# Forming the down weights' combinations early and spooling them, instead of forming them when the MLP starts

## The chip, the cores and the metric

The kernel runs on one core of one Trainium2 chip. The metric is device time in microseconds (us) of one execution. Three runs of the kernel before took 1996.1, 1996.38 and 1999.25 us, so the median is 1996.38 us. The profile that is quoted below is one execution of its own, whose span is 1997.3 us.

Five engines work side by side: TensorE (PE, matrix products), VectorE (DVE), ScalarE (ACT), GpSimd (POOL) and SyncE (SP). In this kernel SP issues every transfer.

## What is computed

The reference is one transformer block with conditioned layer norms, on x of 8192 positions by D = 448 channels:

```
m  = silu(c) @ w_mod                       # six rows: sa, ca, ga, sb, cb, gb
h  = layernorm(x) * (1 + ca) + sa
f  = rfft(h, over the 8192 positions)
f  = soft_shrink(W2 * relu(W1 * f + b1) + b2, 0.01)   # complex, four blocks of 112 channels
x  = x + ga * irfft(f)
h  = layernorm(x) * (1 + cb) + sb
y  = (gelu(h @ w_gate) * (h @ w_up)) @ w_down          # F = 1792 hidden channels
out = x + gb * y
```

The change concerns `w_down`, a matrix of 1792 by 448.

## The kernel before, in words

**Three stages.** Stage A loads x, takes the layer norm statistics and does the first part of the transform. Stage B is a software pipeline of 32 spectral units, `step(0)` to `step(31)`, followed by `drain()`. A unit of about 8.5 us does, for different units at once: `fetch_t` (two transfers `tr<-td` for the unit two steps ahead), `stage_s2` and `stage_m1` (the first complex product), `stage_m2` and `split_y` (the second product; `t` and `y` on DVE, L429 and L437, then `yh` on ACT, L101, and `yl` on POOL, L103), and `stage_i1` (the inverse transform, stored by `vd<-us`). Each exact product uses a high and a low half of its operand, so every operand is split by a cast (high, `zh`, `hh`, `yh`, `th`) and by a subtraction (low, `zl`, `hl`, `yl`, `tl`). The call `at(unit, hook, function)` places other work into a unit. The hook "load" comes right after the unit's fetch and "act" before its `stage_m2`. The hook "dve" comes after its last `split_y` and ahead of `stage_m1`. In this way the units also load and scale `w_gate` and `w_up` (L629, L734, and L743 on DVE in every second unit).

**The seam.** After `drain()` comes a stretch that prepares the first chunk of the MLP: the row ga and the row gb (L609), the last inverse transform (L917 to L919), the residual (L928, L929), statistics, the second norm (`norm2`, L968, L969), the packing into halves (`pack_hi` L974 on ACT, `pack_lo` L981 to L983) and transposes on TensorE (`ptr`, L1001) with their copies (`nt`).

**The MLP.** It runs over 32 chunks of 256 positions. In each chunk `gate_up(i, k)` for k = 0 to 13 does the products with `w_gate` and `w_up` (`pgu`, L1019), then the gelu on ACT (L1055), the product `x` on DVE (L1060), the combinations of `x` on POOL (L1066 to L1069) and the two halves `ac` (L1077 on ACT, L1078 on DVE). A group of output banks in PSUM is reused four values of k later, so TensorE waits for `x` when DVE is late by more than that. At k = 2 of the next chunk `down(i)` multiplies by `w_down` in the Strassen manner: a block of 2 by 2 parts is done with seven products instead of eight. For this each of the seven pairs t of 128-row blocks of `w_down` needs seven matrices of 128 by 224: the four parts, of which three are used as they are, and four combinations of them. Each is needed as a high and a low half in fp16. The fp16 tile `wds[t]` holds them.

**Preparing the next chunk.** While a chunk's `gate_up` runs, the next chunk's inverse, residual, norm, packing and transposes are placed behind certain values of k by a table: `first` for the first chunk, `second` for the second, `hooks` for all the others. The small steps of a reciprocal square root (L112 to L121) are fed one by one between other DVE work.

**The down weights before.** Units 2, 4, ... 14 load `w_down` once (L749) only to take each row's largest absolute value (L753). Units 18 and 19 turn these into one scale per row (`dsc`). The weights are loaded a second time for the preparation proper (L793). For pair t, `parts_hi` (ACT, three instructions, L829 to L831) scales the raw weights and casts the parts. `parts_lo` (six instructions, L835 to L841) subtracts and forms the four combinations. `sums_hi` (ACT, L844) and `sums_lo` (L848) split those. Pairs 0 and 1 are prepared after `drain()` and in the seam, mostly on POOL, and pairs 2 to 6 in the table `first`, on ACT, DVE and POOL, during the first chunk and into the second. The space of the tiles `dr` of L793 comes free only when the seam's last `sums_lo` (DVE, L848) is done.

All transfers stand in one order on SP. They rotate over eight completion semaphores, so a transfer is not issued before the one eight places ahead of it has landed.

Of the kernel before, what the change touches and what calls it, by code (L numbers as in the profile page):

```python
# [43 lines left out]
def spectral_geglu(ctx, tc, x, w1, b1, w2, b2, wg, wu, wd, cvec, wmod, cf1, cs2, cmi, cgm, out):  # L44
# [252 lines left out]
    with ExitStack() as bctx:  # L297
# [493 lines left out]
        def load_d(raw, t):
            raw = raw[:, : 2 * D].rearrange("p (q c) -> p q c", q=2)
            dma(raw, wd.rearrange("(q t p) c -> t p q c", q=2, p=128)[t])  # L793
            return raw

        def load_d4(pool, t):
            draws[t] = load_d(raw_tile(pool).rearrange("p q c -> p (q c)"), t)
# [25 lines left out]
        def quarters(t):  # L823
            r = draws[t]
            return [r[:, q, h * HC : (h + 1) * HC] for q in range(2) for h in range(2)]

        def parts_hi(t):
            r, w = draws[t], wds[t]
            S.activation(r, r, AF.Copy, scale=dsc[:, t : t + 1])  # L829
            S.copy(w[:, 0, 0:2], r[:, :, 0:HC])  # L830
            S.copy(w[:, 0, 2], quarters(t)[3])  # L831

        def parts_lo(t, el=V, add=None):
            w, (b11, b12, b21, b22) = wds[t], quarters(t)
            el.tensor_tensor(w[:, 1, 0:2], draws[t][:, :, 0:HC], w[:, 0, 0:2], ALU.subtract)  # L835
            el.tensor_tensor(w[:, 1, 2], b22, w[:, 0, 2], ALU.subtract)
            add = add or el
            add.tensor_tensor(b11, b12, b11, ALU.subtract)
            add.tensor_tensor(b12, b22, b12, ALU.subtract)
            add.tensor_tensor(b22, b22, b11, ALU.subtract)  # L840
            add.tensor_tensor(b21, b21, b22, ALU.subtract)  # L841

        def sums_hi(t):
            S.copy(wds[t][:, 0, 3:7], draws[t].rearrange("p q (h c) -> p (q h) c", h=2))  # L844

        def sums_lo(t, el=V):
            w, r = wds[t], draws.pop(t).rearrange("p q (h c) -> p (q h) c", h=2)
            el.tensor_tensor(w[:, 1, 3:7], r, w[:, 0, 3:7], ALU.subtract)  # L848

        def down_weights(t, el=V, add=None):  # L850
            parts_hi(t)
            parts_lo(t, el, add)

        def down_weights2(t, el=V):
            sums_hi(t)
            sums_lo(t, el)
# [26 lines left out]
    with ExitStack() as cctx:  # L883
# [265 lines left out]

        first = {  # L1150
            0: [(split_g, 1), (split_v, 1), (parts_hi, 2)],
            2: [(inverse, 1), (parts_hi, 3), (residual, 1), (parts_lo, 2, V, V)],
            3: [(sums_hi, 2), (stats2, 1)],
            4: [(rsqrt_part, 1, 5), (parts_hi, 4), (sums_lo, 2, G), (load_d8, 5), (rsqrt_part, 1, 4)],
            5: [(parts_lo, 3, V, G), (rsqrt_part, 1, 5)],
            7: [(sums_hi, 3), (sums_lo, 3, V), (load_d8, 6)],
            8: [(norm2, 1, 0), (norm2, 1, 1), (parts_lo, 4, G, G), (parts_hi, 5)],
            10: [(pack_hi, 1), (parts_lo, 5, V, V), (pack_lo, 1), (sums_hi, 4)],
            11: [(sums_lo, 4, G), (transposes, 1, 0), (transposes, 1, 2), (sums_hi, 5)],
            12: [(transposes, 1, 4), (sums_lo, 5, G), (parts_hi, 6), (transposes, 1, 6)],  # L1160
            14: [(parts_lo, 6, V, V), (sums_hi, 6)],
            15: [(sums_lo, 6, G)],
        }
# [123 lines left out]
```

## Time and profile before

| what | value |
|---|---|
| runs | 1996.1, 1996.38, 1999.25 us (median 1996.38) |
| profiled execution, span | 1997.3 us |
| TensorE busy | 1930.8 us, 97% of the span |
| DVE, ACT, POOL busy | 1154.4, 772.0, 1190.8 us |
| spectral units | to about 384 us, then the last ones drain |
| seam | about 403 to 424 us |
| chunk 0 of the MLP | about 424 to 474 us |
| steady MLP | from about 510 us |

The busy share of TensorE is close to all of the span, but its ends are modelled. What a stretch really did is better seen from the number of matmuls in it and from the granted clock beside them. A view by windows gives, for each stretch, the busy time of each engine with the number of its instructions in brackets, then the granted TensorE clock (1.00 is full speed), the share of the time in which the transfer engines were busy, and GB/s. A view of waits gives, for each engine and line, the idle time that ended when another engine's instruction ended: the sum, how often, and the longest.

### The profile page before, as it was taken

How to read it: one execution, taken by the hardware profiler on the slowest of the kernel's cores; microseconds unless marked ns; L12 is line 12 of the kernel's file. 1: busy time of each engine (PE TensorE's matmuls, PEld its weight loads, DVE VectorE, ACT ScalarE, POOL GpSimd, SP SyncE). 2: the span in 40 equal slices, each digit the busy share in tenths (PEclk: the TensorE clock that was granted, in tenths of full speed). 3: DMA queues.
4: the chain of work that ended last, by engine and by line, in shares of the span. 5: the costliest groups of instructions: out<-in, count | busy, mean ns of one | idle time of the engine just before them, and what ended most of it. 6: DMA issues, size and time to landing. Idle time of an engine off the chain costs nothing.

```text
span 1997.3 us, 43616 instructions
## 1 busy us (share of the span) xinstructions
PE 1930.8 (97%) x17678; PEld 1712.6 (86%) x17678; DVE 1154.4 (58%) x2419; ACT 772.0 (39%) x1307; POOL 1190.8 (60%) x1478
## 2 busy tenths in 40 slices
PE   7889989987999999999999999999999999999999
PEld 3588989966898888888888888888888888889898
DVE  8468888867555555555554555555555555555533
ACT  5555667653333333333333333333333333333322
POOL 3234446557666666666666666666666666666644
PEclk9889999988999999999999999999999999999999
DMA  9996657721111111111111111111111111111000
GB/s 351 325 227 173 170 147 198 192 89 46 47 44 43 43 43 43 44 49 42 42 49 47 42 42 42 42 51 42 42 42 42 42 43 43 43 43 43 22 17 19
DMA packets 165697, 157.72 MB, mean 79 GB/s; under 512 B 86516, under 2 KB 146552, under 8 KB 165496
## 3 DMA queue, kind: packets, MB, share of 16 engines
q1 hardware_dynamic: 165496, 154.95, 27.4%
q8 instruction: 138, 2.26, 0.5%
q14 instruction: 63, 0.52, 0.1%
HBM read 95.09 MB, written 44.04 MB: 70 GB/s over the span
## 4 chain that ended last, share of the span: by engine, by line
PE 83%; DVE 8%; DMA 4%; ACT 2%; SPq 1%; POOL 1%; issue 1%; DVEq 0%; ACTq 0%; POOLq 0%
PE pgu L1019 51%; PE pdn L1087 7%; PE pdn L1085 7%; PE pdn L1086 7%; DVE y L437 2%; PE ps L194 1%; DMA xt<-in_A_x 1%; DMA raw<-in_B_w_up 1%; DVE zl L352 1%; DMA td<-xt 1%; PE pi L919 1%; DVE hl L407 1%; DVE t L429 1%; PE pi L917 1%; PE pi L918 1%
## 5 line engine op out<-in xcount | busy, mean ns | idle before, releaser
L1019 PE MATMUL pgu<-nt,wh 128*128 128x256 f16 x6272 | 835.2, 273 | 1.2 <-DVE x L1060 1.2
L1019 PEld LDWEIGHTS <-wh 128*128 128x128 f16 x6272 | 603.2, 98 | 99.4 <-issue 31.3
L1055 ACT ACTIVATE gel<-pgu,dg 128x256 f32<-128x256 f32 x448 | 199.8, 471 | 789.8 <-PE pgu L1019 750.0
L1019 PE MATMUL pgu<-nt,wl 128*128 128x256 f16 (+1 forms) x3584 | 502.6, 273 | 0.5 <-DVE x L1060 0.4
L1085 PE MATMUL pdn<-wd,ac 128*128 128x224 f16 x1568 | 407.8, 260 | 4.3 <-DVE x L928 2.3
L1087 PE MATMUL pdn<-wd,ac 128*128 128x224 f16 x1568 | 407.8, 260 | 0.2 <-DVE ac L1078 0.2
L1086 PE MATMUL pdn<-wd,ac 128*128 128x224 f16 x1568 | 407.7, 260 | 0.0
L1066 POOL TENSOR_TENSOR x<-x 128x128 f32<-128x128 f32 x223 | 240.2, 1077 | 234.6 <-DVE x L1060 234.6
L1078 DVE SCALAR_TENSOR_TENSOR ac<-x,sa_act,ac 128x896 f16<-128x896 f32 (+1 forms) x225 | 311.6, 1385 | 81.8 <-ACT ac L1077 81.8
L1019 PEld LDWEIGHTS <-wl 128*128 128x128 f16 (+1 forms) x3584 | 298.2, 97 | 58.3 <-issue 24.8
L1060 DVE TENSOR_TENSOR x<-pgu,gel 128x256 f32<-128x256 f32 x448 | 179.4, 418 | 282.9 <-ACT gel L1055 282.2
L1077 ACT ACTIVATE ac<-x,sa_act 128x896 f16<-128x896 f32 (+1 forms) x225 | 233.0, 1035 | 53.1 <-POOL x L1069 51.2
L1120 POOL TENSOR_TENSOR o<-u,p 128x224 f32<-128x224 f32 x32 | 21.0, 656 | 292.8 <-DVE u L1119 292.8
L1067 POOL TENSOR_TENSOR x<-x 128x128 f32<-128x128 f32 x223 | 158.4, 710 | 17.5
L1086 PEld LDWEIGHTS <-ac 128*128 128x128 f16 x1568 | 154.1, 98 | 5.5 <-issue 4.7
L1085 PEld LDWEIGHTS <-ac 128*128 128x128 f16 x1568 | 154.0, 98 | 1.0 <-issue 0.2
L1087 PEld LDWEIGHTS <-ac 128*128 128x128 f16 x1568 | 154.0, 98 | 0.9 <-DVE ac L1078 0.5
L103 POOL TENSOR_TENSOR yl<-y,yh 128x448 fp32r<-128x448 f32 x63 | 75.3, 1196 | 89.1 <-ACT yh L101 86.8
L1068 POOL TENSOR_TENSOR x<-x 128x128 f32<-128x128 f32 x223 | 112.2, 503 | 0.0
L103 POOL TENSOR_TENSOR tl<-tr,th 128x896 f16<-128x896 f32 x30 | 57.3, 1909 | 87.5 <-ACT th L101 74.4
L1069 POOL TENSOR_TENSOR x<-x 128x128 f32<-128x128 f32 x223 | 108.0, 484 | 0.0
L437 DVE TENSOR_TENSOR y<-pm,t 64x224 f32<-64x224 f32 x256 | 99.5, 389 | 8.1
(305 smaller groups left out, 2835.7 us busy)
## 6 DMA issues: line engine op xcount, KB each, us to landing
tr<-td SPq DMA_DIRECT2D x64, 224.0 KB, 4.8
vd<-us SPq DMA_DIRECT2D x64, 224.0 KB, 3.0
xx<-in_A_x SPq DMA_DIRECT2D x32, 448.0 KB, 3.4
v<-vd SPq DMA_DIRECT2D x64, 224.0 KB, 2.9
out<-x SPq DMA_DIRECT2D x31, 448.0 KB, 2.6
xt<-in_A_x SPq DMA_DIRECT2D x15, 896.0 KB, 17.5
nt<-pk SPq DMA_TRANSPOSE x480, 2.3
td<-xt SPq DMA_DIRECT2D x8, 896.0 KB, 15.7
```

Of the source, the lines that this page charges most:

```text
L103: (el or V).tensor_tensor(lo, src, h, ALU.subtract)
L437: V.tensor_tensor(y[ri * 64 : ri * 64 + 64, gi], pv[si, ri], tv[si, ri], ALU.subtract)
L1019: T.matmul(pgu[i, t, q][:, pr * H : (pr + 1) * H], w[rows, tw, f0 : f0 + 128], nts[i][rows, tn, :], start=start, stop=stop, skip_group_che ...
L1055: S.activation(gl, ps[:, :H], AF.Gelu_apprx_tanh, scale=dg)
L1060: V.tensor_tensor(dst, ps[:, H : 2 * H].rearrange("p (b c) -> p b c", b=2), gl.rearrange("p (b c) -> p b c", b=2), ALU.mult)
L1066: e.tensor_tensor(s1, a21, a22, ALU.add)
L1067: e.tensor_tensor(s2, s1, a11, ALU.subtract)
L1077: S.activation(ac[:, 0, k], x[:, k], AF.Copy, scale=sc)
L1078: V.scalar_tensor_tensor(ac[:, 1, k], x[:, k], sc, ac[:, 0, k], op0=ALU.mult, op1=ALU.subtract)
L1085: T.matmul(ps, ac[:, 0, ka], wds[t][:, 0, kb], start=t == 0, stop=False)
L1086: T.matmul(ps, ac[:, 0, ka], wds[t][:, 1, kb], start=False, stop=False)
L1087: T.matmul(ps, ac[:, 1, ka], wds[t][:, 0, kb], start=False, stop=t == NP - 1)
```

## The change

The combinations are now formed in fp32 from the raw weights during units 4 to 16, before any scale is known, and stored.

- A new DRAM buffer `wdd` holds for each of the seven pairs a block of 128 by 7 by 224 in fp32 (784 KB). `load_m` loads the four parts of a pair by three transfers into a tile `m`, in units 4, 6, 7, 9, 11, 12 and 14. One unit later `down_sums` takes the row maximum on DVE (over 896 values to one column, where two columns were made before) and forms the four combinations on POOL. One more unit later `store_m` stores all seven matrices to `wdd`.
- The preparation of a pair is then a load of its block (`load_d`), one ACT instruction `down_hi` (scale and cast of 128 by 1568) and one DVE instruction `down_lo` (scale and subtract of 128 by 1568).
- For pairs 0 to 2 (`ND = 3`) these are placed in units 22 and 23, 25 and 26, 28 and 29. For pairs 3 to 6 they are placed in the table `first`, by k. Nothing of the down weights is left between `drain()` and the first chunk except two loads.
- The table `first` is rearranged: the next chunk's norm comes at k = 5 and 6 (before at 8), the packing at 6 and 8 (before at 10), the transposes at 10, 11 and 12 (before at 11 and 12).
- Two of the four combinations change places in the block, so two products in `down` swap their index. The number of matmuls stays.
- The scratch space that the program sets aside for software-generated transfers is made smaller. All of the kernel's transfers are of the hardware kind.

```diff
+ND = 3
+    wdd = dram.tile([NP, 128, 7, HC], F32, name="wdd")
...
-            raw = raw_tile(pool).rearrange("p q c -> p (q c)")[:, : 2 * D].rearrange("p (q c) -> p q c", q=2)
-            dma(raw, wd[j * 256 : (j + 1) * 256, :].rearrange("(q p) c -> p q c", p=128))
+            m = pool.tile([128, 7, HC], F32, tag="m", name="m", bufs=4)
+            r = wd.rearrange("(q t p) c -> t p q c", q=2, p=128)[t]
+            dma(m[:, 0:2], r[:, :, :HC])
+            dma(m[:, 3], r[:, 0, HC:])
+            dma(m[:, 2], r[:, 1, HC:])
...
+        def down_sums(t):
+            m = raws[("m", t)]
             V.tensor_reduce(
-                dn[:, 2 * j : 2 * j + 2], raws.pop(("m", j)), mybir.AxisListType.X, ALU.max, apply_absolute_value=True
+                dn[:, t : t + 1], m[:, 0:4].rearrange("p q c -> p (q c)"), mybir.AxisListType.X, ALU.max, apply_absolute_value=True
             )
+            b11, b21, b22, b12, c1, c4, c3 = (m[:, j] for j in range(7))
+            G.tensor_tensor(c1, b12, b11, ALU.subtract)
+            G.tensor_tensor(c3, b22, c1, ALU.subtract)
+            G.tensor_tensor(c4, b21, c3, ALU.subtract)
+            G.tensor_tensor(b12, b22, b12, ALU.subtract)
+        def store_m(t):
+            dma(wdd[t], raws.pop(("m", t)))
...
-        for j in range(7):
-            at(2 + 2 * j, "load", pre, npool, ("m", j), load_m, j)
-            at(3 + 2 * j, "dve", down_max, j)
+        for t, n in enumerate((4, 6, 7, 9, 11, 12, 14)):
+            at(n, "load", pre, npool, ("m", t), load_m, t)
+            at(n + 1, "dve", down_sums, t)
+            at(n + 2, "load", store_m, t)
...
+        def load_d(pool, t, bufs):
+            draws[t] = pool.tile([128, 7, HC], F32, tag="dr", name="dr", bufs=bufs)
+            dma(draws[t], wdd[t])
...
+        def down_hi(t):
+            assert not tiny
+            S.activation(wds[t][:, 0], draws[t], AF.Copy, scale=dsc[:, t : t + 1])
+        def down_lo(t):
+            w = wds[t]
+            V.scalar_tensor_tensor(w[:, 1], draws.pop(t), dsc[:, t : t + 1], w[:, 0], op0=ALU.mult, op1=ALU.subtract)
...
-        for t in range(2):
-            at(30 + t, "load", load_d4, fp, t)
+        for t in range(ND):
+            at(22 + 3 * t, "load", load_d, fp, t, 1)
+            at(23 + 3 * t, "act", down_hi, t)
+            at(23 + 3 * t, "dve", down_lo, t)
...
-        down_weights(0, G)
...
-        down_weights2(0, G)
-        down_weights(1, G)
...
-        for t in (2, 3, 4):
-            load_d8(t)
+        for t in range(ND, ND + 2):
+            load_d(cp2, t, 2)
...
-        down_weights2(1)
...
+        first = {
+            0: [(split_g, 1), (split_v, 1), (down_hi, 3)],
+            1: [(down_lo, 3)],
+            2: [(inverse, 1), (residual, 1)],
+            3: [(stats2, 1), (load_d, cp2, 5, 2)],
+            4: [(rsqrt_part, 1, 14)],
+            5: [(norm2, 1, 0), (down_hi, 4)],
+            6: [(norm2, 1, 1), (pack_hi, 1)],
+            7: [(down_lo, 4), (load_d, cp2, 6, 2)],
+            8: [(pack_lo, 1), (down_hi, 5)],
+            9: [(down_lo, 5)],
+            10: [(transposes, 1, 0), (transposes, 1, 2), (down_hi, 6)],
+            11: [(transposes, 1, 4), (down_lo, 6)],
+            12: [(transposes, 1, 6)],
+        }
```

**Where it moves instructions.** In the early units, SP's order after the change reads as follows around units 14 to 16. The names `tr`, `s`, `raw` and `vd` are those of the units, and L752 to L754 are `load_m` of the last pair:

```order
L313 DMA tr<-td 64x4x224 x2
L319 DMA s_2602<-cs 128x1024
L631 DMA raw<-in_B_w_up 128x3x256
L633 DMA raw<-in_B_w_up 64x256 x2
L752 DMA m<-in_B_w_down 128x2x224
L753 DMA m<-in_B_w_down 128x224
L754 DMA m<-in_B_w_down 128x224
L473 DMA vd<-us 64x896 x2
L313 DMA tr<-td 64x4x224 x2
L631 DMA raw<-in_B_w_gate 128x3x256
L633 DMA raw<-in_B_w_gate 64x256 x2
L769 DMA wdd<-m 128x1568
```

Where the one transfer `raw<-in_B_w_down` of L749 stood there are now three, and a store of 784 KB stands before the next units' `vd` and `tr`. On POOL the same pair adds four instructions behind a unit's last `yl` and ahead of the next `tl`:

```order
L105 TENSOR_TENSOR yl<-y,yh 128x448 x2
L763 TENSOR_TENSOR m<-m 128x224
L764 TENSOR_TENSOR m<-m 128x224
L765 TENSOR_TENSOR m<-m 128x224
L766 TENSOR_TENSOR m<-m 128x224
L105 TENSOR_TENSOR tl<-tr,th 128x896
```

In unit 26, DVE's order after the change has `down_lo` (L840) between the unit's last `y` and the next `hl`, beside the `wl` that stood there already:

```order
L431 TENSOR_SCALAR t<-pm_4762 128x448
L439 TENSOR_TENSOR y<-pm_4762,t 64x224 x4
L744 SCALAR_TENSOR_TENSOR wl<-raw,sw,wh 128x4x256
L840 SCALAR_TENSOR_TENSOR wd_3389<-dr,dsc,wd_3389 128x1568
L409 SCALAR_TENSOR_TENSOR hl<-pm_4801,hh_800 112x2x256
L409 SCALAR_TENSOR_TENSOR hl<-pm_4817,hh_801 112x2x256
```

In units 23 and 29 the same instruction is new there without the `wl`.

In chunk 0 DVE's order was, before, from the first `x` on (`pi` is the next chunk's inverse):

```order
L1060 TENSOR_TENSOR x_5910<-pgu,gel 128x2x128
L928 TENSOR_TENSOR x_5923<-pi_5912,ga_r 128x448
L928 TENSOR_TENSOR x_5923<-pi_5916,ga_r 128x448
L835 TENSOR_TENSOR wd_5677<-dr,wd_5677 128x448
L836 TENSOR_TENSOR wd_5677<-dr,wd_5677 128x224
L838 TENSOR_TENSOR dr<-dr 128x224
L839 TENSOR_TENSOR dr<-dr 128x224
L840 TENSOR_TENSOR dr<-dr 128x224
L841 TENSOR_TENSOR dr<-dr 128x224
L1060 TENSOR_TENSOR x_5910<-pgu,gel 128x256
L1078 SCALAR_TENSOR_TENSOR ac<-x_5879,sa_act,ac 128x896
```

and is, after the change:

```order
L1046 TENSOR_TENSOR x_5910<-pgu,gel 128x256
L840 SCALAR_TENSOR_TENSOR wd_5726<-dr,dsc,wd_5726 128x1568
L1046 TENSOR_TENSOR x_5942<-pgu,gel 128x2x128
L914 TENSOR_TENSOR x_5952<-pi_5944,ga_r 128x448
L914 TENSOR_TENSOR x_5952<-pi_5948,ga_r 128x448
L1046 TENSOR_TENSOR x_5942<-pgu,gel 128x256
L1064 SCALAR_TENSOR_TENSOR ac<-x_5910,sa_act,ac 128x896
```

One instruction stands for the six of `parts_lo`, and the later `sums_lo` of the pair is gone too. Here, and in the rest of chunk 0, POOL's list no longer holds an instruction of the down weights.

More of the change, by code (lines that the diff above doesn't have):

```diff
@@ L80, in spectral_geglu @@
     rmax = cpool.tile([128, 2], F32, name="rmax")
-    dn = cpool.tile([128, NFT], F32, name="dn")
+    dn = cpool.tile([128, NP], F32, name="dn")
     dsc = cpool.tile([128, NP], F32, name="dsc")
@@ L716, in down_scales @@
         def down_scales():
-            VL.tensor_tensor(dsc, dn[:, :NP], dn[:, NP:], ALU.max)
-            VL.tensor_tensor(dsc, dsc, isa, ALU.mult)
+            VL.tensor_tensor(dsc, dn, isa, ALU.mult)
             VL.tensor_reduce(hs, dsc, mybir.AxisListType.X, ALU.max)
@@ L745, in weights_lo, with load_m @@
                 G.tensor_tensor(wl[:, :, fs], raw, wh[:, :, fs], ALU.subtract)
-        def load_m(pool, j):
-            raw = raw_tile(pool).rearrange("p q c -> p (q c)")[:, : 2 * D].rearrange("p (q c) -> p q c", q=2)
-            dma(raw, wd[j * 256 : (j + 1) * 256, :].rearrange("(q p) c -> p q c", p=128))
-            return raw
-        def down_max(j):
+        def load_m(pool, t):
+            m = pool.tile([128, 7, HC], F32, tag="m", name="m", bufs=4)
[3 more added lines that the diff above has]
+            dma(m[:, 2], r[:, 1, HC:])
+            return m
+        def down_sums(t):
+            m = raws[("m", t)]
             V.tensor_reduce(
-                dn[:, 2 * j : 2 * j + 2], raws.pop(("m", j)), mybir.AxisListType.X, ALU.max, apply_absolute_value=True
+                dn[:, t : t + 1], m[:, 0:4].rearrange("p q c -> p (q c)"), mybir.AxisListType.X, ALU.max, apply_absolute_value=True
             )
+            b11, b21, b22, b12, c1, c4, c3 = (m[:, j] for j in range(7))
[5 more added lines that the diff above has]
+            dma(wdd[t], raws.pop(("m", t)))
         nctx = ExitStack()
@@ L783, in spectral_geglu @@
         ep = ctx.enter_context(tc.tile_pool(name="ep", bufs=1))
-        wds = [ep.tile([128, 2, 7, HC], F16, name=f"wd{t}") for t in range(1)]
+        wds = [ep.tile([128, 2, 7, HC], F16, name=f"wd{t}") for t in range(ND)]
         draws, nxt = {}, {}
[L791 to L797, printed above, removed]
+        def load_d(pool, t, bufs):
+            draws[t] = pool.tile([128, 7, HC], F32, tag="dr", name="dr", bufs=bufs)
+            dma(draws[t], wdd[t])
         def load_g(i):
@@ L821, in split_g, with down_weights @@
             nxt[i]["g"] = gh, gl
[L823 to L856, printed above, removed]
+        def down_hi(t):
[4 more added lines that the diff above has]
+            V.scalar_tensor_tensor(w[:, 1], draws.pop(t), dsc[:, t : t + 1], w[:, 0], op0=ALU.mult, op1=ALU.subtract)
+        def down_weights(t):
+            down_hi(t)
+            down_lo(t)
         fctx = ExitStack()
@@ L891, in x8 @@
             return cp.tile([128, 8, 128], F32, tag="x8", name="x8", bufs=3)
-        def load_d8(t):
-            draws[t] = load_d(cp2.tile([128, 2 * D], F32, tag="dr", name="dr", bufs=3), t)
         def each(i):
@@ L1115, in down @@
             V.tensor_tensor(u2, product(i, bank("pd", "pdn"), 4, 6), p1, ALU.add)
-            V.tensor_tensor(u4, product(i, bank("pd", "pdn"), 3, 3), u2, ALU.add)
-            p7 = product(i, bank("pd", "pdn"), 5, 4)
+            V.tensor_tensor(u4, product(i, bank("pd", "pdn"), 3, 4), u2, ALU.add)
+            p7 = product(i, bank("pd", "pdn"), 5, 3)
             V.tensor_tensor(o22, p7, u4, ALU.add)
@@ L1148, in spectral_geglu @@
         }
[L1150 to L1163, printed above, removed]
         dma(nxt[0]["v"][:, :, HC:], vd[1, :CB].rearrange("b q c -> q b c"))
@@ L1267 @@
     from concourse.bass_utils import run_bass_kernel_spmd as _run
-    nc = _bacc.Bacc("TRN2", target_bir_lowering=False, num_devices=1)
+    nc = _bacc.Bacc("TRN2", target_bir_lowering=False, num_devices=1, dynamic_dma_scratch_size=1024)
     arrays, args = {}, []
```

## The prediction

> **What bounds the kernel now.** I read the page's head and its chain first, then windows of equal length, then TensorE's waits in the stretch that the windows point to. The page and its chain:
>
> ```profile
> span 1997.3 us, 43616 instructions
> PE 83%; DVE 8%; DMA 4%; ACT 2%; SPq 1%; POOL 1%; issue 1%; DVEq 0%; ACTq 0%; POOLq 0%
> ```
>
> TensorE sets the time nearly everywhere, and the change leaves its matmuls as they are. It can only gain where TensorE waits, or is granted less clock, and lose where it makes TensorE wait. Windows over the seam, chunk 0, the first `down` and the steady MLP:
>
> ```profile
> 408.00:434.00 26.00, 20.39 (x122) 16.32 (x123) 17.00 (x38) 13.03 (x24) 11.60 (x12) 0.80 0.33 104
> 434.00:474.00 40.00, 29.94 (x259) 24.15 (x256) 34.18 (x57) 21.65 (x35) 34.54 (x42) 0.87 0.16 50
> 482.00:502.00 20.00, 15.66 (x123) 13.74 (x123) 12.93 (x32) 3.77 (x6) 7.12 (x8) 0.83 0.21 58
> 600.00:640.00 40.00, 40.00 (x378) 34.73 (x376) 24.12 (x48) 15.48 (x25) 30.86 (x40) 1.00 0.16 47
> ```
>
> Steady state does 378 matmuls in 40 us. Chunk 0 did 259, so 40 x (1 - 259/378) = 12.6 us were lost there, at a clock of 0.87. From 482 to 502 us, 123 were done where 189 would be steady: 7.0 us lost. The waits of 400 to 510 us say on whom:
>
> ```profile
> PE ptr L1001 <- ACT pk L974: 6.5, 3, 5.3
> PE pi L919 <- DVE vl L103: 3.2, 3, 2.8
> PE ptr L1001 <- POOL pk L981: 3.2, 1, 3.2
> PE pdn L1085 <- DVE x L928: 2.3, 1, 2.3
> PE pdn L1085 <- DVE u L1115: 2.1, 1, 2.1
> PE pgu L1019 <- DVE x L1060: 1.6, 2, 1.2
> ```
>
> Waits of 5.3 + 3.2 + 1.6 = 10.1 us in chunk 0 leave 2.5 of the 12.6 to the clock. The names ACT and POOL mislead: the cast `pk` waits for `norm2`, which is late on DVE, busy 34.18 of 40 us. So in chunk 0 the bound is DVE, with POOL (34.54) beside it.
>
> **Chunk 0.** On DVE the pieces of the down weights cost, up to 474 us:
>
> ```profile
> L836 DVE TENSOR_TENSOR wd<-dr,wd 128x224 f16<-128x224 f32 x3 | 2.6, 865 | 0.0
> L835 DVE TENSOR_TENSOR wd<-dr,wd 128x448 f16<-128x448 f32 x3 | 2.4, 788 | 0.0
> L838 DVE TENSOR_TENSOR dr<-dr 128x224 f32<-128x224 f32 x2 | 1.9, 974 | 0.0
> L848 DVE TENSOR_TENSOR wd<-dr,wd 128x896 f16<-128x896 f32 x1 | 1.3, 1303 | 1.5 <-ACT wd L844 1.5
> L839 DVE TENSOR_TENSOR dr<-dr 128x224 f32<-128x224 f32 x2 | 0.9, 460 | 0.1
> L840 DVE TENSOR_TENSOR dr<-dr 128x224 f32<-128x224 f32 x2 | 0.9, 459 | 0.1
> L841 DVE TENSOR_TENSOR dr<-dr 128x224 f32<-128x224 f32 x2 | 0.9, 446 | 0.1
> ```
>
> together 10.9 us. They go, and four `down_lo` come. No row has that shape. The nearest are of the same kind with fewer elements, in the units and in the MLP, and for `down_hi` on ACT:
>
> ```profile
> L743 DVE SCALAR_TENSOR_TENSOR wl<-raw,sw,wh 128x1024 f16<-128x1024 f32 x4 | 5.1, 1284 | 0.1
> L1078 DVE SCALAR_TENSOR_TENSOR ac<-x,sa_act,ac 128x896 f16<-128x896 f32 x5 | 7.9, 1580 | 0.0
> L734 ACT ACTIVATE wh<-raw,sw 128x1024 f16<-128x1024 f32 x5 | 5.9, 1177 | 0.0
> ```
>
> By L743 one `down_lo` is 1284 x 1568/1024 = 1.97 us. By L1078 in chunk 0, where POOL crowds it, it is 1580 x 1568/896 = 2.77. I take 1.97, the nearer shape, and keep 2.77 for the range. `down_hi` is 1177 x 1568/1024 = 1.80 us, about what the replaced casts of a pair cost, and ACT is busy 21.65 of 40. DVE's work in chunk 0 becomes 34.2 - 10.9 + 4 x 1.97 = 31.2 us.
>
> When can it start? The rows of SP's load of `dr`, of ACT's use of it, of DVE's first `x`, and of the TensorE instruction that the load waits for after the change:
>
> ```profile
> 426.36 19.64 SPq L793 DMA_DIRECT2D dr<-in_B_w_down  x4
> 430.02 1.04 ACT L829 ACTIVATE dr<-dr,dsc 128x896 f32<-128x896 f32 x1 [3.72 <-DMA dr<-in_B_w_down]
> 433.76 0.79 DVE L1060 TENSOR_TENSOR x<-pgu,gel 128x256 f32<-128x256 f32 x2 [6.64 <-ACT gel L1055]
> 415.14 5.50 PE L609 MATMUL psm<-raw,cs 112*128 112x224 f32 x16
> ```
>
> The load of `dr` was held until DVE's L848 was done, ACT waited 3.72 us for it, and the first gelu and `x` were queued behind it. After the change the load waits only for TensorE's L609, some 6 us earlier. The 784 KB take 784/448 x 3.6 = 6.3 us at most if I scale the 430.02 - 426.36 = 3.6 us of before. So `down_hi` runs near 426, and `x` starts near 429 instead of 433.76, by then with TensorE about 2.5 us earlier too (next part).
>
> Without any loss chunk 0 would end at 474 - 12.6 - 2.5 = 459 us. DVE then has 30 us for its 31.2. It stays nearly full, and what it is late is TensorE's wait: 1.2 us by this count. The order adds some, since `pack_hi` stands on ACT ahead of a gelu and waits for the second `norm2`. I take **2 us** left over. The bounds are 0 (if POOL's departure makes DVE's shared instructions shorter) and 1.2 + 4 x 0.8 = 4.4 (by L1078's price). Chunk 0: -12.6 + 2.0 = **-10.6**.
>
> [...] L969 took 685 ns in the seam and 1150 in chunk 0, the same shape:
>
> ```profile
> L969 DVE SCALAR_TENSOR_TENSOR n<-n,r,sb_r 128x448 f32<-128x448 f32 x2 | 1.4, 685 | 0.1
> L969 DVE SCALAR_TENSOR_TENSOR n<-n,rcy,sb_r 128x448 f32<-128x448 f32 x2 | 2.3, 1150 | 0.1
> ```
>
> [...]
>
> **The seam.** All eight ACT, one DVE and thirteen POOL instructions of pairs 0 and 1 leave it. What that frees on the path is the second pair of `vl`:
>
> ```profile
> 412.02 2.71 DVE L103 TENSOR_TENSOR vl<-v,vh 128x224 fp32r<-128x224 f32 x2
> 411.46 1.88 POOL L848 TENSOR_TENSOR wd<-raw,wd 128x896 f16<-128x896 f32 x1 [1.77 <-ACT wd L844]
> 410.39 0.39 DVE L929 TENSOR_TENSOR x<-x,xx 128x224 f32<-128x224 f32 x1
> ```
>
> While POOL ran L848, two of them took 2.71 us. An instruction of that size takes 0.39, and TensorE waited 2.8 us for them. So 2.71 - 0.8 = 1.9 us, and about 0.6 for the clock, granted at 0.80 in this stretch: **-2.5** (bounds -1 to -4).
>
> **The first `down`.** The wait for DVE's `x` of L928 came behind `parts_lo` of the last pair, which moves ahead of it. The one for `u` of L1115 stays, since what stands before it stays. Of 7.0 us lost, its share by the two waits is 7.0 x 2.3/4.4 = **-3.7** (bounds 0 and -4).
>
> **Units 23, 26 and 29.** Here the additions meet a full machine. Windows of two neighbouring units and DVE's idle time over eight:
>
> ```profile
> 305.40:313.98 8.58, 8.49 (x81) 8.20 (x80) 8.19 (x16) 6.21 (x11) 5.11 (x5) 1.00 0.66 173
> 313.98:322.36 8.38, 8.38 (x81) 8.16 (x79) 6.88 (x16) 6.90 (x12) 5.87 (x4) 1.00 0.74 197
> L407 DVE SCALAR_TENSOR_TENSOR hl<-pm,hh 112x512 fp32r<-112x512 f32 x16 | 10.3, 686 | 4.9 <-ACT hh L406 4.7
> ```
>
> TensorE has nothing to spare. DVE's slack before `hl` is 4.9/4 = 1.2 us in each of the four units without `wl`. Units with `wl` (1.28 us, same place) have used it up and are 0.15 us longer. So `down_lo` costs 1.97 - 1.2 = 0.8 us in units 23 and 29, and nearly all of its 1.97 in unit 26: **+3.5**. The floor is 0, if a delayed `hl` has cover in TensorE's queue. The ceiling is 3 x 1.97 = 5.9. ACT's 1.80 delays the same `hh` by less than DVE delays `hl` (ACT was busy 6.9 of 8.4), and the two delays lie side by side.
>
> **Units 4 to 16.** Each pair adds four POOL instructions. The nearest rows and the load on the transfers:
>
> ```profile
> L838 POOL TENSOR_TENSOR raw<-raw 128x224 f32<-128x224 f32 x2 | 1.5, 734 | 0.0
> L841 POOL TENSOR_TENSOR dr<-dr 128x224 f32<-128x224 f32 x2 | 2.8, 1387 | 0.2
> L103 POOL TENSOR_TENSOR tl<-tr,th 128x896 f16<-128x896 f32 x13 | 24.8, 1909 | 30.2 <-ACT th L101 25.2 <-DMA tr<-td 5.0
> 130.00:140.00 10.00, 10.00 (x96) 9.77 (x95) 8.21 (x17) 7.00 (x13) 4.74 (x4) 1.00 1.05 227
> ```
>
> At 734 to 1387 ns, four are 2.9 to 5.5 us a pair. POOL is idle for over 5 of 10 us, 30.2/13 = 2.3 us of it just before `tl`, where they stand, and `tl` is wanted only in the next unit. The row maximum reads as many values as before. The stores add 7 x 784 KB over some 120 us, about 45 GB/s on the 227 of this window. TensorE was busy all the time there, at a transfer share of 1.05. I take **+0.3** (bounds 0 and 5).
>
> **Sum.** -10.6 - 2.5 - 3.7 + 3.5 + 0.3 = -13.0, on the profiled 1997.3: 1984.3. The median of the runs lies 0.9 below that execution, so I predict **1983.5 us**.
>
> **Rivals.**
> 1. DVE stays the bound of chunk 0. `down_lo` at 2.77 and more, with rsqrt and two `norm2` packed into k = 4 to 6, brings the wait for `pk` back in part. The 34.18 of 40 speak for it, POOL's departure against. It keeps half of chunk 0's loss (+4.3) and, since DVE is then late for the first `down` too, nothing of the -3.7 is won: 1983.5 + 8 = 1991.5. [...]
> 2. Everything added is covered: units at 0 to +1, nothing left in chunk 0: 1983.5 - 3 - 2 = 1978.5. For it speaks that a unit's results are wanted a unit later; against it the 0.15 us that a `wl` costs.
> 3. Slower. `store_m` stands on SP ahead of the next `vd` and `tr`, and the transfer eight places behind it waits until it has landed:
>
> ```profile
> td<-xt SPq DMA_DIRECT2D x8, 896.0 KB, 15.7
> tr<-td SPq DMA_DIRECT2D x64, 224.0 KB, 4.8
> ```
>
> By the larger store's rate one of 784 KB lands in 15.7 x 784/896 = 13.7 us, and the transfer eight places on is due a unit, about 8.8 us, later. That holds SP for some 4 us, and POOL's combinations ahead of the store for up to 3 more. `tr` is fetched about one unit ahead of its split: 8.8 - 4.8 = 4 us of cover. Past that point each further us is TensorE's; if the hold is 7 us a pair, 7 x 3 = 21: 2004. Against it: those long landings belong to a stretch with several large transfers at once.
>
> **Chances.** The forecast has 0.60, the first rival 0.20, the second 0.10, the third 0.10. The range has to reach the second rival and the first: **1977 to 1994**. A difference of 0.2% (4 us) is about what this kernel's runs can tell from none. Faster by more than that takes the forecast, the second rival and most of the first: 0.86; within it 0.06, from the end of the first; slower 0.08, the third where its hold is long.
>
> **What would show it.** Right: in chunk 0 TensorE's wait for `pk` is gone or under 3 us, chunk 1 starts near 461 us plus what the units cost, `vl` takes 0.8 us a pair, `x` of L928 no longer holds the first `down`, and units 23 and 29 are 0.8 and unit 26 nearly 2 us longer. Wrong: a `pk` wait of 4 us or more with `down_lo` over 2.7, or TensorE waiting for `tr` or for `yl` in units 6 to 17.

## The result, and the profile after

The changed kernel ran in 1986.13, 1987.23, 1987.67 and 1988.25 us, median 1987.45. The kernel before, with one run more, had a median of 1997.52. The ratio is 0.9947, with a 95% interval of [0.9933, 0.9961]: 10 us faster, where 13 had been predicted. The ratios below are likewise to runs of the kernel before that were timed beside it (medians 1998.93 us for runs 1, 4 and 5, and 1998.31 us for runs 6, 7 and 9). The profiled execution has a span of 1986.5 us against 1997.3, so 10.8 us less.

The windows and TensorE's waits of the changed kernel, over the stretches that answer to chunk 0 and the first `down` (columns as before):

```profile
span 1986.5 us, 43631 instructions
430.00:470.00 40.00, 36.36 (x340) 30.50 (x338) 28.96 (x48) 22.12 (x31) 27.04 (x31) 1.00 0.24 82
477.00:497.00 20.00, 18.03 (x166) 16.83 (x165) 10.58 (x32) 1.53 (x3) 6.97 (x10) 0.91 0.23 65
PE pi L903 <- ACT vh L103: 3.3, 2, 1.9
PE ptr L987 <- ACT pk L960: 2.0, 2, 1.1
PE pdn L1071 <- ACT p L1100: 2.0, 1, 2.0
PE pgu L1005 <- DVE nt L996: 1.8, 2, 1.6
PE ptr L987 <- POOL pk L967: 1.2, 1, 1.2
PE ptr L987 <- DVE nt L996: 0.8, 1, 0.8
```

Chunk 0 now does 340 matmuls in its first 40 us, at full clock. The 259 of the prediction come from a window that begins 10 us into the chunk. The first 40 us of chunk 0 held 279 before:

```profile
423.90:463.90 40.00, 32.41 (x279) 26.32 (x276) 30.48 (x52) 22.49 (x36) 28.16 (x32) 0.93 0.26 85
```

The two long waits for `pk` in chunk 0 (5.3 and 3.2 us) are one of 1.2. New are short waits for the copies `nt`, which stand behind a `down_lo` on DVE.

Set side by side, the two traces give a ledger by stages. Its marks are the drain's last `pi` matmul with `yl` (one more matmul follows it), TensorE's first gate matmul, and the first matmul of `down`:

```profile
402.24 0.47 PE L467 MATMUL pi<-yl,mih 128*128 128x448 f32 x1 [0.19 <-DVE yl L103]
423.93 1.70 PE L1019 MATMUL pgu<-nt,wh 128*128 128x256 f16 x7
482.65 0.27 PE L1085 MATMUL pdn<-wd,ac 128*128 128x224 f16 x1
```

before, and after the change:

```profile
412.03 0.47 PE L469 MATMUL pi<-yl,mih 128*128 128x448 f32 x1 [0.19 <-DVE yl L105]
429.86 0.71 PE L1005 MATMUL pgu<-nt,wh 128*128 128x256 f16 x5
477.40 0.27 PE L1071 MATMUL pdn<-wd,ac 128*128 128x224 f16 x1
```

| stage | before | after | difference | predicted |
|---|---|---|---|---|
| start to that `pi` | 402.24 | 412.03 | +9.8 | +3.8 |
| seam, to the first gate matmul | 21.69 | 17.83 | -3.9 | -2.5 |
| chunk 0 and the next, to the first `down` | 58.72 | 47.54 | -11.2 | -10.6 |
| from there to the end of the span | 1514.65 | 1509.10 | -5.6 | -3.7 |
| sum | 1997.3 | 1986.5 | -10.8 | -13.0 |

So the total came out near, but through two misses of opposite sign, and that they nearly cancel is luck. The units cost 6 us more than was computed, and the rest gained 4 us more.

Part of the last stage is spread and not the change. From the first `down` to the start of chunk 2 it fell from 49.4 to 45.2 us, which is -4.2. The other -1.4 lie in chunks 2 to 31. Two kernels of the experiments (runs 2 and 3) have the old code there, and in their profiles that part is 2.1 and 1.6 us shorter than in the profile of the kernel before. The experiments were made on the cost of the units, and on what sets chunk 0.

The place of the extra cost is seen when DVE's first `t` of each unit is compared between the two traces. Up to unit 3 the changed kernel is 1.9 us ahead. Then it loses 2.7 us from unit 8 to unit 11, 2.2 in unit 15, 0.8 by unit 22 and 0.5 elsewhere. It loses 0.9 in unit 23, 2.6 in unit 26, 1.1 in unit 27 and 0.9 in unit 29. Units 26 and 15 look like this. First unit 26 (DVE, then TensorE's clock in windows of 2 us, third number from the end of a row):

```profile
349.15 1.28 DVE L744 SCALAR_TENSOR_TENSOR wl<-raw,sw,wh 128x1024 f16<-128x1024 f32 x1
350.35 2.72 DVE L840 SCALAR_TENSOR_TENSOR wd<-dr,dsc,wd 128x1568 f16<-128x1568 f32 x1
353.11 1.29 DVE L409 SCALAR_TENSOR_TENSOR hl<-pm,hh 112x512 fp32r<-112x512 f32 x2
...
352.00:354.00 2.00, 0.15 (x1) 0.15 (x2) 1.97 (x3) 1.97 (x3) 1.18 (x1) 1.00 1.04 258
356.00:358.00 2.00, 2.00 (x9) 1.92 (x9) 1.82 (x6) 0.00 (x0) 0.00 (x0) 0.50 0.04 12
358.00:360.00 2.00, 2.00 (x12) 1.86 (x11) 1.85 (x5) 1.63 (x3) 1.15 (x1) 0.78 0.00 0
```

`down_lo` took 2.72 us here and not the 1.97 of the sum. TensorE waited 2.7 us for `hl`, and from 355.5 us on, 1.6 us behind the end of that wait, it was granted half its clock for 3.4 us. That second part was in no term of the sum. Now unit 15, DVE and POOL of the changed kernel:

```profile
243.11 0.61 DVE L484 TENSOR_SCALAR nrm<-nrm 128x28 int32<-128x28 int32 x1
244.29 1.92 DVE L484 TENSOR_SCALAR nrm<-nrm 128x28 int32<-128x28 int32 x1
243.02 0.67 POOL L765 TENSOR_TENSOR m<-m 128x224 f32<-128x224 f32 x1
244.27 1.91 POOL L105 TENSOR_TENSOR tl<-tr,th 128x896 f16<-128x896 f32 x1
```

Two small DVE instructions of the weights' norms, 0.17 us each in the kernel before, end with the POOL instruction beside them: 243.11 + 0.61 = 243.72 and 243.02 + 0.67 = 243.69, then 244.29 + 1.92 = 246.21 and 244.27 + 1.91 = 246.18. POOL's four combinations had pushed `tl` onto them.

### The profile page after: what moved, and what is told of

The parts are those of the page before. It is cut to its first block, busy times and chain, and to the rows that moved or that the text cites. A ratio compares the mean times of both kernels' runs of the same rounds, so it can differ in the third digit from the quotient of the medians.

```text
span 1986.5 us, 43631 instructions
## 1 busy us (share of the span) xinstructions
PE 1927.5 (97%) x17678; PEld 1715.7 (86%) x17678; DVE 1143.9 (58%) x2403; ACT 765.3 (39%) x1286; POOL 1185.1 (60%) x1479
## 4 chain that ended last, share of the span: by engine, by line
PE 85%; DVE 7%; DMA 4%; ACT 2%; SPq 1%; issue 1%; POOL 1%; ACTq 0%; DVEq 0%
PE pgu L1005 51%; PE pdn L1073 7%; PE pdn L1071 7%; PE pdn L1072 7%; DVE y L439 2%; DMA xt<-in_A_x 1%; PE ps L196 1%; DMA td<-xt 1%; DVE zl L354 1%; PE pi L905 1%; PE pi L903 1%; PE pi L904 1%; DMA raw<-in_B_w_up 1%; DVE t L431 1%; DVE hl L409 1%
```

## The experiments

Theory A: the extra cost is the change's own, made of a small instruction held by POOL (unit 15), of `down_lo` and `wl` in one unit, and of the half clock that follows a wait. Rivals: the low clock falls by chance; the stores and loads of `wdd` are what lengthens the units.

**1. The changed kernel once more**, with no edit.

> The changed kernel once more, unaltered. In its profile the drain was reached 9.8 us later than before, where 3.8 were predicted, and TensorE's clock fell to 0.50 for about 4 us each near 182, 196, 295 and 356 us, places at which it stayed at 1.00 before. Theory A (each wait of TensorE of about a microsecond or more, placed by the program, brings such a stretch, so it belongs to the change): the stretches recur at the same places within a few us, the drain is again reached 9 to 10 us later, the time is 1986 to 1988. Theory B (the stretches fall by chance): at least two of the four are gone or elsewhere, and the drain moves by 3 us or more against the first profile.

Median 1989.12 us (1984.39 to 1990.23), ratio 0.9947 [0.9932, 0.9962], span 1988.2. Units 15, 23, 26, 27 and 29 cost the same as in the first profile within 0.1 us, and the stretches near 296 and 358 us came again. Those near 182 and 196 did not, though the waits of 0.8 and 1.3 us stood there again: units 8 to 11 lost 0.7 us in place of 2.7. Over all eight profiles that have the new early part, these stretches came in four. So 2 us of this part are chance. The recorded expectation is met by neither theory in full. Two of the four stretches are gone, as B said, but the drain came 1.7 us later than in the first profile and not 3 or more away from it, and it came 11.5 us later than before, where A said 9 to 10.

The stretch near 296 us is not the change's either. Runs 2 and 3 have the old code up to there and no dummy yet, and they show one at 284.7 to 288.1 and at 287.8 to 291.2 us. The profile of the kernel before happens to have none there. The first units vary too: at unit 3 these eight profiles stood between 2.6 us ahead and 1.6 us behind the kernel before, so the 1.9 us that the first profile seemed to win there cannot be put down to the change. Both belong to the spread of this kernel's times.

**2. The price of a DVE instruction at that place.** The kernel before, with a dummy reduction in the hook of `down_lo`:

```diff
+        dd = cpool.tile([128, 8], F32, name="dd")
...
+        def delay(r, n):
+            V.tensor_reduce(
+                dd[:, :r], cb_r[:, :n].unsqueeze(1).to_broadcast([128, r, n]), mybir.AxisListType.X, ALU.max, apply_absolute_value=True
+            )
...
+        for n, (r, c) in zip((21, 23, 25, 27, 29), ((2, 410), (3, 416), (4, 420), (5, 424), (6, 426))):
+            at(n, "dve", delay, r, c)
```

> The kernel before with one dummy DVE instruction (a reduction whose result nothing uses) added where down_lo stands, in units 21, 23, 25, 27 and 29, of about 1.0, 1.5, 2.0, 2.5 and 3.0 us. These units had 1.2 us of DVE slack. Prediction's price (duration minus 1.2, nothing else): 0, 0.3, 0.8, 1.3 and 1.8 us, 4.2 together. Theory A (a wait above some length also brings a stretch at half clock): the first two or three as priced, and from some dose on 1.5 to 2 us more than priced with clock 0.50 for about 4 us behind it, 6 to 8 us together. Rival C (a delayed hl has cover in TensorE's queue): below 2 us together.

The shortest and the longest of the five dummies, and TensorE's waits behind the last four:

```profile
301.58 1.00 DVE L870 TENSOR_REDUCE dd<-cb_r 128x2 f32<-128x820 f32 x1
371.54 2.82 DVE L870 TENSOR_REDUCE dd<-cb_r 128x6 f32<-128x2556 f32 x1
320.66 0.37 PE L418 MATMUL pm<-w2h,hl 112*128 112x224 f32 x1 [0.27 <-DVE hl L407]
338.36 0.37 PE L418 MATMUL pm<-w2h,hl 112*128 112x224 f32 x1 [0.72 <-DVE hl L407]
356.52 0.37 PE L418 MATMUL pm<-w2h,hl 112*128 112x224 f32 x1 [1.18 <-DVE hl L407]
375.13 0.37 PE L418 MATMUL pm<-w2h,hl 112*128 112x224 f32 x1 [1.63 <-DVE hl L407]
```

Durations of 1.00, 1.45, 1.90, 2.36 and 2.82 us gave waits of none, 0.27, 0.72, 1.18 and 1.63: duration minus 1.2, to 0.1 us. The prediction's rule for the price holds. Behind the last one came a stretch at 0.50 (376.9 to 380.3 us) and 1.2 us more. The one timed run took 2001.97 us. This dose run alone could not say whether the length of the wait or the moment brings it.

**3. The same dose five times.** The kernel before with the longest dummy in all five units:

```diff
-        for n, (r, c) in zip((21, 23, 25, 27, 29), ((2, 410), (3, 416), (4, 420), (5, 424), (6, 426))):
+        for n, (r, c) in zip((21, 23, 25, 27, 29), ((6, 426),) * 5):
```

> The kernel before with the longest dummy DVE instruction of the dose run (2.82 us, which made TensorE wait 1.6 us and was followed once by 4 us at half clock) in all five units 21, 23, 25, 27 and 29. By duration minus 1.2 each unit costs 1.6 us, 8.1 together. Theory A (a single wait of that length brings the half clock): a stretch at 0.50 behind each of the five, 1.2 us more each, 14 together. Theory A2 (such a wait brings it only at some moments): behind one to three of the five, 9 to 12 us together.

From unit 21 to unit 31 it lost 11.8 us. The windows in which the clock would show it, behind the doses of units 21, 23, 25, 27 and 29:

```profile
306.00:308.00 2.00, 2.00 (x11) 2.00 (x11) 1.35 (x3) 0.19 (x1) 1.35 (x1) 0.50 0.82 253
328.00:330.00 2.00, 2.00 (x15) 1.89 (x14) 1.85 (x5) 0.00 (x0) 0.35 (x1) 1.00 0.70 238
346.00:348.00 2.00, 2.00 (x11) 2.00 (x11) 1.88 (x4) 0.00 (x0) 0.98 (x1) 0.50 0.98 272
366.00:368.00 2.00, 2.00 (x16) 1.92 (x15) 1.86 (x5) 0.00 (x0) 0.52 (x1) 1.00 0.86 260
386.00:388.00 2.00, 2.00 (x16) 1.92 (x15) 1.84 (x5) 0.89 (x2) 0.24 (x1) 1.00 0.02 8
```

Behind two of five equal doses the clock fell, for 6.8 and for 3.4 us, and these two cost 2.5 and 0.9 us more than the others. TensorE's waits for `hl` there were 2.00 and 1.62 us. In units 23 and 27 they were 1.28 each, and in unit 29 TensorE was idle for 1.64 us between 380 and 384 us. So behind a wait of about 1.6 us the half clock came at one moment and not at another (A2). Here it is a surcharge with a chance, not a fixed price. The one timed run took 2008.95 us, against 2000.38 for the kernel before beside it.

**4. No `down_lo` in a unit that has `wl`.**

```diff
-        for t in range(ND):
-            at(22 + 3 * t, "load", load_d, fp, t, 1)
-            at(23 + 3 * t, "act", down_hi, t)
-            at(23 + 3 * t, "dve", down_lo, t)
+        for t, n in enumerate((23, 27, 29)):
+            at(n - 1, "load", load_d, fp, t, 1)
+            at(n, "act", down_hi, t)
+            at(n, "dve", down_lo, t)
```

> The changed kernel with the split of the second pair moved from unit 26 to unit 27, so that down_lo no longer stands in a unit that has wl on DVE. In the changed kernel units 26 and 27 together were 3.7 us longer than before, and units 23 and 29 0.9 each. Theory A: unit 27 costs 0.9 like the other two, the half-clock stretch near 356 us is gone, the time falls by 2.8 us to about 1984.5. Rival D (it is the load of dr and the traffic, or ACT, that lengthens these units): no change, within 1 us.

Unit 26 is back at its old length and unit 27 costs 0.9 us. Together that is 2.8 us less than in the changed kernel, as expected. The wait sums of this kernel and of the changed one, from 312 to 400 us:

```profile
PE pm L420 <- DVE hl L409: 2.5, 3, 0.8
...
PE pm L420 <- DVE hl L409: 4.4, 3, 2.7
```

The longest wait fell from 2.7 to 0.8 us, and no window behind it shows a low clock. The timed runs do not resolve it: 1987.16 us (1984.57 to 1992.03), ratio 0.9949 [0.9929, 0.9968], as for the changed kernel. The span of its profile is 1983.6.

**5. The last pair's combinations one unit earlier.**

```diff
-        for t, n in enumerate((4, 6, 7, 9, 11, 12, 14)):
+        for t, n in enumerate((4, 6, 7, 9, 11, 12, 13)):
```

> The changed kernel with load, combinations and store of the seventh pair one unit earlier (units 13, 14, 15 in place of 14, 15, 16). In unit 15 two small DVE instructions (nrm, 128x28) took 0.61 and 1.92 us in place of 0.17 each, lying exactly beside POOL's combinations and the tl that these had pushed back, and the unit was 2.2 us longer than before. Theory E (DVE's small instructions are held by POOL's): unit 15 goes back to about 8.9 us, nrm to 0.2, the time falls by about 2 us. Rival F (the store or the transfers in front of fetches lengthen that unit): unit 14 or 15 stays 2 us too long, since the transfers only move by a unit.

In unit 15 the two `nrm` instructions are short again:

```profile
242.73 0.17 DVE L484 TENSOR_SCALAR nrm<-nrm 128x28 int32<-128x28 int32 x1
243.47 0.17 DVE L484 TENSOR_SCALAR nrm<-nrm 128x28 int32<-128x28 int32 x1
```

The unit is 9.0 us long (8.9 before), and units 3 to 20 together cost nothing (-0.1 us at unit 3, -0.2 at unit 20). In this sum 0.7 us are lost in units 8 to 11, as in the repeat, and 0.8 are won in unit 17. That 0.8 is chance: runs 2 and 3, with the old code there, won it too, and in all three a stretch at half clock lasted 3.4 us there and not 6.8 as in the profile of the kernel before. Median 1984.12 us (1983.0 to 1985.53), ratio 0.9927 [0.9912, 0.9942], an interval that overlaps that of the changed kernel. All transfers and stores are still there, so rival F falls. The stores were hidden in the changed kernel as well: they landed in 4.4 us (the median), and TensorE waited for no transfer in units 6 to 17.

```profile
wdd<-m SPq DMA_DIRECT2D x7, 784.0 KB, 4.4
tr<-td SPq DMA_DIRECT2D x25, 224.0 KB, 4.5
SPq L769 <- POOL m L766: 3.4, 4, 2.2
```

**6. Halves that fit the slack.** Pairs 0 and 1 in two pieces each, pair 2 beside the row ga:

```diff
+        cut = (slice(0, 4), slice(4, 7))
...
+            V.scalar_tensor_tensor(w[:, 1, cut[q]], r[:, cut[q]], dsc[:, t : t + 1], w[:, 0, cut[q]], op0=ALU.mult, op1=ALU.subtract)
...
-        for t in range(ND):
-            at(22 + 3 * t, "load", load_d, fp, t, 1)
-            at(23 + 3 * t, "act", down_hi, t)
-            at(23 + 3 * t, "dve", down_lo, t)
+        for t, n in enumerate((23, 27)):
+            at(n - 1, "load", load_d, fp, t, 1)
+            for q in range(2):
+                at(n + 2 * q, "act", half_hi, t, q)
+                at(n + 2 * q, "dve", half_lo, t, q)
+        at(30, "load", load_d, fp, 2, 1)
...
         drain()
+        down_weights(2)
         mod_row("ga", ga_r)
```

> The changed kernel with the splits of pairs 0 and 1 cut in two (four of the seven matrices, then three) in units 23, 25 and 27, 29, and pair 2 split after the drain, beside the row ga. The dummy instructions have shown a price of duration minus 1.2 us in such a unit. Halves of 1.15 and 0.87 us lie below it. Theory A: units 22 to 30 cost 0 to 0.5 in place of 5.5 us, no half-clock stretch near 356, and pair 2's 1.6 on ACT and 2.0 on DVE lie in the 5 us in which DVE waited there, so the time falls by 5 us against the changed kernel. Rival D (the loads of dr and ACT's share lengthen the units): 2 us or more stay in units 23 to 30. Rival G: pair 2 delays ga_r and vl, and the seam gives back 2 us or more.

From unit 22 to the drain it lost 0.0 us, where the changed kernel lost 5.5. A half took 1036 ns in the mean, and DVE's idle time before `hl` went down instead of TensorE's work:

```profile
L863 DVE SCALAR_TENSOR_TENSOR wd<-dr,dsc,wd 128x896 f16<-128x896 f32 (+1 forms) x4 | 4.1, 1036 | 0.1
L409 DVE SCALAR_TENSOR_TENSOR hl<-pm,hh 112x512 fp32r<-112x512 f32 x16 | 10.3, 687 | 0.7 <-ACT hh L408 0.5
```

Rival D falls with that: the three loads of `dr`, and ACT's work for pairs 0 and 1, were still in the units. The seam took 18.8 us. Six profiles without pair 2 there have 17.8 to 18.4 us, so pair 2 gave back between 0.4 and 1 us. Median 1980.32 us (1978.37 to 1985.16), ratio 0.9912 [0.9895, 0.993]. Part of the difference to the changed kernel is chance, since this profile had no half clock in units 8 to 11.

**7. The old order in chunk 0.** Norm, packing and transposes of the next chunk back at their old values of k, all else as changed:

```diff
-            5: [(norm2, 1, 0), (down_hi, 4)],
-            6: [(norm2, 1, 1), (pack_hi, 1)],
+            5: [(down_hi, 4)],
             7: [(down_lo, 4), (load_d, cp2, 6, 2)],
-            8: [(pack_lo, 1), (down_hi, 5)],
+            8: [(norm2, 1, 0), (norm2, 1, 1), (down_hi, 5)],
             9: [(down_lo, 5)],
-            10: [(transposes, 1, 0), (transposes, 1, 2), (down_hi, 6)],
-            11: [(transposes, 1, 4), (down_lo, 6)],
-            12: [(transposes, 1, 6)],
+            10: [(pack_hi, 1), (pack_lo, 1), (down_hi, 6)],
+            11: [(transposes, 1, 0), (transposes, 1, 2), (down_lo, 6)],
+            12: [(transposes, 1, 4), (transposes, 1, 6)],
```

> The changed kernel with the next chunk's norm, packing and transposes put back to the values of k that they had before (norm2 at 8, packing at 10, transposes at 11 and 12). Chunk 0 (from its first gate matmul to the next chunk's first) took 50.2 us before and 38.0 after. Theory H (the gain there is the work taken off DVE and POOL, the order is secondary): it stays below 42 us, TensorE's wait for pk is 1 to 4 us. Rival I (the gain is the earlier place of norm and packing): most of it goes, 46 us or more, with a wait for pk of 6 us or more.

From the first gate matmul to the first `down` it took 47.57 us, against 47.54 in the changed kernel. The waits only change names:

```profile
PE ptr L987 <- POOL pk L967: 3.0, 1, 3.0
PE ptr L987 <- DVE nt L996: 0.7, 1, 0.7
```

The end of chunk 0 came 1.7 us later, and the next chunk made that up before its `down`. So the new order wins nothing by itself, and the gain in chunk 0 comes from the work that was taken away and from what that sets free. Median 1988.21 us, ratio 0.9947 [0.9931, 0.9964].

**8. Twice the `down_lo` in chunk 0.**

```diff
-            w = wds[t]
-            V.scalar_tensor_tensor(w[:, 1], draws.pop(t), dsc[:, t : t + 1], w[:, 0], op0=ALU.mult, op1=ALU.subtract)
+            w, r = wds[t], draws.pop(t)
+            for _ in range(1 if t < ND else 2):
+                V.scalar_tensor_tensor(w[:, 1], r, dsc[:, t : t + 1], w[:, 0], op0=ALU.mult, op1=ALU.subtract)
```

> The changed kernel with each of the four down_lo of chunk 0 issued twice in a row (the second repeats the first), 8 us more on DVE there. In the changed kernel TensorE still lost 3.6 us in chunk 0 while DVE was busy 29 of 40 us. Theory J (DVE still sets chunk 0, as the prediction had it): chunk 0 grows by 5 to 9 us. Rival K (its remaining waits are only single instructions standing in front of a copy or a packing; DVE has room): by 1 to 4 us.

53.70 us to the first `down`, 6.2 more for 8 us of work. To the next chunk's first gate matmul, the mark of the recorded expectation, it is 4.6 more, between the 5 to 9 of theory J and the 1 to 4 of rival K:

```profile
PE pgu L1006 <- DVE nt L997: 3.3, 2, 3.1
PE ptr L988 <- POOL pk L968: 3.2, 1, 3.2
PE ptr L988 <- DVE nt L997: 1.4, 1, 1.4
```

Three quarters of this added DVE work reach TensorE. So DVE still counts in chunk 0 of the changed kernel, though it is busy only 28.96 of 40 us there: the idle time lies at its beginning, before the first gelu, and in single waits for `gel` and `ac`. The one timed run took 1992.03 us.

**9. The three findings together.** The halves of run 6, run 5's earlier pair, and in chunk 0 `pack_lo` directly behind `pack_hi` and the last two `down_lo` behind the transposes:

```diff
-        for t, n in enumerate((4, 6, 7, 9, 11, 12, 14)):
+        for t, n in enumerate((4, 6, 7, 9, 11, 12, 13)):
...
-            6: [(norm2, 1, 1), (pack_hi, 1)],
+            6: [(norm2, 1, 1), (pack_hi, 1), (pack_lo, 1)],
...
-            8: [(pack_lo, 1), (down_hi, 5)],
-            9: [(down_lo, 5)],
-            10: [(transposes, 1, 0), (transposes, 1, 2), (down_hi, 6)],
-            11: [(transposes, 1, 4), (down_lo, 6)],
-            12: [(transposes, 1, 6)],
+            8: [(down_hi, 5)],
+            10: [(transposes, 1, 0), (transposes, 1, 2)],
+            11: [(transposes, 1, 4)],
+            12: [(transposes, 1, 6), (down_lo, 5)],
+            13: [(down_hi, 6)],
+            14: [(down_lo, 6)],
```

> The halves of the first kernel of this call, the combinations of the seventh pair one unit earlier (that took 2.2 us out of unit 15), and in chunk 0 pack_lo directly behind pack_hi, and the splits of pairs 5 and 6 behind the transposes, so that no down_lo stands ahead of an nt copy. Theory: 5 us (units) + 2.5 (unit 15 and what follows) + 2.5 of the 3.6 left in chunk 0 = 10 us below the changed kernel, about 1977. Rival: the three gains share what they win and 1981 to 1984 is seen.

Median 1978.52 us (1976.63 to 1982.08), ratio to the kernel before 0.9902 [0.9887, 0.9917]: it beats both the kernel before and the changed kernel. From unit 3 to the drain it loses 0.7 us in all. Chunk 0 gained only 0.7 us of the 2.5 expected (46.84 us to the first `down`), since the copy on ACT and the next `vl` on POOL became what TensorE waits for:

```profile
PE ptr L1000 <- ACT nt L1011: 2.1, 2, 1.7
PE pi L918 <- POOL vl L105: 1.3, 1, 1.3
```

## Why the prediction came out, step by step

**Chunk 0: right in size, shared out only in part.** -10.6 predicted, -11.2 measured to the first `down` (-12.2 to the end of chunk 0, since a wait of 1.6 us for `nt` falls into the next one), with 3.6 us of waits left where 2 had been taken. `down_lo` took 1.84 to 2.05 us there, as scaled from L743, and not the 2.77 of the upper bound. The first rival (DVE keeps half of the loss) did not happen. Run 7 shows that the order does not carry the gain, and run 8 that added DVE work reaches TensorE at three quarters of its length. But DVE's work on the down weights fell only from 10.9 to 8.0 us, which at that rate is worth some 2 us. The rest came with three other things: the earlier start that the prediction had worked out, the half clock that is gone (10.2 us long before, from 460.7 us on), and POOL's departure. DVE's first `x` came 5.90 us behind the first gate matmul, where it had been 9.83:

```profile
435.76 0.79 DVE L1046 TENSOR_TENSOR x<-pgu,gel 128x256 f32<-128x256 f32 x2 [4.10 <-ACT gel L1041]
```

No run separates these three.

**The seam: right, somewhat larger.** The second pair of `vl` went from 2.71 us to 0.69 as the step said, and the stage won 3.9 us (3.3 in the repeat) where 2.5 had been taken and 4 was the bound.

**The first `down`: right, near its bound.** -3.7 predicted, with a bound of -4. Measured are -4.2 up to chunk 2. The -5.6 of the table hold 1.4 more from chunks 2 to 31, which is no more than the spread of the old code there. The wait for `x` of L928 is gone. The other one stays at 2.0 us under another name, as said. In the kernel before each of the two waits had a stretch at half clock of 3.4 us behind it, and after the change one is left.

**Units 23, 26 and 29: the rule was right, the size not.** +3.5 predicted, +5.5 measured. Units 23 and 29 cost 0.9 each (0.8 predicted). Runs 2 and 6 show the rule itself, duration minus 1.2 us of slack. In unit 26 two terms were missing: `down_lo` took 2.72 us (+0.7; POOL's `yl` had started 0.5 us before it, while in unit 23 `down_lo` started first and took 2.02), and the wait of 2.7 us was followed by a stretch at half clock (+1.1). The row for the half clock was in the profile before, and the prediction used it in the seam and in chunk 0, but not for the waits that the change itself makes.

**Units 4 to 16: the step that failed.** It priced POOL's combinations at +0.3, by looking at who waits for POOL: `tl` and `yl`, and these were indeed not missed. It did not look at which small DVE instructions would run beside them. In unit 15 that cost 2.2 us (run 5 takes it away). The profile before had a case of it, in chunk 0. There a step of the reciprocal square root on 128 by 2 values took 1.81 us, ending with a POOL instruction of the down weights (after the change such a step takes 0.17):

```profile
443.82 1.81 DVE L113 TENSOR_SCALAR rcy<-rcve 128x2 int32<-128x2 int32 x1
443.71 1.89 POOL L848 TENSOR_TENSOR wd<-dr,wd 128x896 f16<-128x896 f32 x1
```

Another 2 us in units 8 to 11 was the chance of the half clock (run 1). The cause of the 0.7 us that all eight profiles lose there stays open. The bound of 5 us had been left open for transfers, which cost nothing.

The 0.8 us that units 20 and 21 lost come in every profile with the change, and with them the stretch at half clock near 296 us. Runs 2 and 3, with the old code, lose 0.6 and 1.5 us in unit 20, with such a stretch too. So this loss is not shown to be the change's.

**The third rival** (stores hold SP) did not happen: SP waited 3.4 us for POOL at four of the stores together, and the stores landed in 4.4 us, not in 13.7. The long landings of the row that was used (15.7 us) are those of the first stage, as the argument against it said.

## What to carry to other kernels

Before work is put into a full pipeline, read off the slack of the engine at that very place (idle time before one named instruction, divided by how often it occurs) and cut the work into pieces below it: in run 2 the price was duration minus slack to a tenth of a microsecond. Two pairs in halves, in units without `wl`, cost nothing, where three wholes, one of them beside a `wl`, cost 5.5 us. When work is given to GpSimd, look not only at who waits for GpSimd but also at which VectorE instructions will run beside it, the small ones among them: here two of 0.17 us took 0.61 and 1.92. And a wait that an edit creates on TensorE should be priced with a possible stretch at half clock behind it, worth 0.9 to 2.5 us here.

## What the runs showed of the hardware

Two small VectorE instructions that take 0.17 us otherwise took 1.92 us (the changed kernel, unit 15) and 1.81 us (the kernel before, chunk 0), and both ended 0.03 us behind the end of the GpSimd instruction beside them. Not every small one did so. In the kernel before, `mx` of L482 began at 243.44 us, while a `tl` ran on POOL from 242.95 to 244.86 us, and took 0.17 us. A GpSimd instruction took longer as well: in unit 23 `down_lo` had started first and took 2.02 us, and POOL's `yl`, started 0.7 us behind it, took 2.31 us, where the `yl` before it took 1.15. Why one instruction was longer beside the other and another was not, no run shows.

A granted clock of 0.50 for 3.4 us (6.8 with the first of the five equal doses) came in or within 2 us behind single waits of TensorE of 1.6 to 2.7 us, at some moments and not at others: with the wait of 1.63 us of run 2 and those of 2.00 and 1.62 us of run 3, and with none of the waits of 0.27, 0.72 and 1.18 us of run 2 and of 1.28, 1.28 and about 1.6 us of run 3. In unit 20 the kernel before waited 1.63 us and had no such stretch behind it, and run 3, with the same code up to there, had one from 287.8 us on. In units 8 to 11 it came, in four profiles of eight, behind groups of shorter waits (0.8 and 1.3 us in the changed kernel). Windows of 2 us cover 112 to 294 us in all eleven traces, and more in most. In them the stretches at 0.50 begin whole multiples of 3.413 us apart within each trace, to 0.04 us, and last 3.4, 6.8 or 10.2 us. What decides whether a wait has such a stretch behind it, no run shows.
